# Two linear-attention blocks mixed by a gate, on one core: weight loads, W' work and denominator work placed differently around the last transposes

## The chip, the cores and the metric

The kernel runs on one NeuronCore of one Trainium2 chip. The metric is device microseconds for one execution. TensorE (PE in the profile; its weight loads are PEld) does the matrix products, VectorE (DVE) and ScalarE (ACT) the elementwise work, GpSimd (POOL) some memsets, and the sync engine (SP) issues nearly all DMAs from one in-order queue (SPq).

## The reference, cut to what matters

Two blocks A and B have the same input `x` (2048 x 640, bf16) and weights of their own. `phi` is an ELU-like feature map, H is 32 heads of 20 columns.

```python
x = A_x
g = _sigmoid((x * gate_w).sum(-1, keepdims=True))
qkv = x @ wqkv;  q, k, v = three parts, 32 heads of 20
phi = lambda t: jnp.where(t > 0, t + 1, jnp.exp(t)) + 1e-6
pq, pk = phi(q), phi(k)
kv = jnp.einsum("bhsd,bhse->bhde", pk, v)
z = jnp.einsum("bhsd->bhd", pk)
num = jnp.einsum("bhqd,bhde->bhqe", pq, kv)
den = jnp.einsum("bhqd,bhd->bhq", pq, z)[..., None] + 1e-6
a = (num / den).reshape(B, S, D) @ wo        # and b likewise, with B's weights
return g * a + (1 - g) * b
```

## The kernel before, in words

**Stages.** (1) k-units: for each of 16 row tiles, `x` times both k weights (L557, L558), then exp, relu and add on ACT and DVE. (2) Five g-units (`g_unit`, L814): G = pkᵀx for both blocks in seven products of eight matmuls each, P1 to P7 (L806), with a Strassen-like combination on DVE and ACT; beside them runs the query work of the row blocks 0 and 1 (`q_unit`, L762). A row block is 512 rows; there are four. Each g-unit ends with two DMA transposes, `gsA` and `gsB`, from the tile WKW into GSA and GSB. (3) `kv_unit` (L924): G times the v weights gives the per-head kv; three masked copies on DVE (L904) make the tile KVL. (4) `wp_burst` (L957): kv times `wo` gives W' for each block in two halves; each half leaves PSUM by two copies of 124 x 960 (L972), and after the second half five DMAs store W' to DRAM (`st`, L988), and one DMA (`wplA`, `wplB`) loads it back in the order in which the output products need it. (5) Output: for each of 16 row tiles, 20 matmuls (L1116; the first ten read A's W', the others B's), a copy (L1140) and a store.

**The denominator.** For each row block b, `t_sum` (L1007) adds up, on DVE, five products of query features with z per attention block: the first is a multiply-add (L1016, g = 0), the others take the sum so far along (L1022). `den(b)` (L1031) then transposes the sums by DMA (`tt`), reduces them (L1049), takes the reciprocal (L1061), multiplies by the gate and spreads each factor over four columns in one instruction (L1064), transposes that back by DMA (`fx`) and scales the query features in two halves (L1094, "pqs"). Output tiles 4b to 4b+3 need pqs of block b.

**What sets the order.** The kernel is written as a list of operations with dependencies, and a planner (`Sched.run`, L99) places them at build time: on each engine it takes the operation that can start first by its own cost figures, and among those that can start, the one with the lowest `prio`. `prio` is the place in the program's text unless it is given; the weight loads discussed here have −1. PE is the exception: its operations stay in the order of the text. At run time every engine and the SP queue work through that fixed order, each instruction behind the one in front of it. The first loads carry a `behind` link (L370) that keeps them in order among themselves; `can` (L110) refuses an operation whose `behind` has not been placed. An operation with no dependencies can start at the planner's first moment, 300 ns, like the first load of `x`.

**Placing of the loads and of the query work.** `fill_g` (L1174) is called four times within each g-unit (k = 0 to 3). In the last g-unit it calls `load_wv` at k = 0 (v weights A and B, 800 KB each, waiting for the products P1 and P2, whose tiles they overwrite), and `load_wo` at k = 1 (eight DMAs, 1650 KB together, waiting for P6 and P2). Query units 2 and 3 of the row blocks come as ten "double" units of two PSUM banks each (two exps and relus of 1024 columns, L784 and L785; L788 and L794 on DVE). L1193 to L1222 set their order: two doubles, kv, one, W' A half 0, one, `den(1)`, W' A half 1, one, W' B half 0, one, W' B half 1, three, the first products of two output tiles, one more double inside the output loop, then `den(2)`, `den(3)`. `den(0)` stands ahead of all of these.

Of the kernel before, what the change touches and what calls it, by code (L numbers as in the profile page):

```python
# [42 lines left out]
HC = 320  # L43
RELUB = (3, 5, 7, 9, 11, 13)
QPRE = 2
QO = 3
NEA = 2
QFILL = ((3, 2, 1, 1), (0, 1, 1, 1), (0, 1, 1, 1), (0, 1, 1, 1), (0, 1, 1, 0))

# [222 lines left out]
def body(nc, A_x, A_wqkv, A_wo, B_x, B_wqkv, B_wo, gate_w, out, log=None):  # L272
# [26 lines left out]
    ONE = sb("ONE", [128, 2], bf)  # L299
    SCR = sb("SCR", [128, 1], f32)  # L300
    EPSC = sb("EPSC", [128, 1], f32)
    IDN = sb("IDN", [128, 128], bf)
    PS = nc.alloc_psum_tensor("ps", [128, 8, 512], f32)

# [23 lines left out]

    base = RA1 * RL
    WVW = D + 28  # L330
    WV = {X: PKf[:, base + i * NC * WVW : base + (i + 1) * NC * WVW].rearrange("p (c f) -> p c f", c=NC) for i, X in enumerate(XS)}
    base += 2 * NC * WVW
    WO = {X: PKf[:, base + i * NU * D : base + (i + 1) * NU * D].rearrange("p (u f) -> p u f", u=NU) for i, X in enumerate(XS)}
    assert base + 2 * NU * D <= (RS2 + 1) * RL
    PQ23 = PKf[:, RS1 * RL : RS1 * RL + 4 * 2560].rearrange("p (b k s) -> p b k s", b=2, k=10)
# [47 lines left out]
    def dve2(n):  # L383
        return 150 + 0.53 * n
# [12 lines left out]

    op("DVE", lambda e: e.memset(ONE[:, :], 1.0), 60.0, outs=[bone], name="one")
    sch.consts = [op("POOL", lambda e: e.memset(EPSC[:, :], EPS), 100.0, outs=[beps], name="eps")]
    op("ACT", lambda e: e.activation(SCR[:, :], EPSC[:, :], ACT.Exp), 1500.0, ins=[beps], outs=[bge0], prio=10**6, name="table")  # L400
    bid = Buf("idn")
    op(
# [49 lines left out]
    loading.clear()  # L452

    bpad = {X: Buf("pad") for X in XS}

    def load_wv(after):
        for X in XS:
            for lo, hi in ((0, 4), (D + 4, D + 28)):
                op("POOL", lambda e, X=X, lo=lo, hi=hi: e.memset(WV[X][:, :, lo:hi], 0.0), 300.0, outs=[bpad[X]], after=after, name="wvpad")
            dma("SP", "wv" + X, WV[X][:, :, 4 : D + 4], w3(X, 2), 819200, outs=[bwv[X]], after=after, prio=-1)  # L460

    def load_wo(after):
        for X in XS:
            for r in range(2):
                bwo[X, r] = Buf("wo")
                dma(
                    "SP",
                    "wo%s%d" % (X, r),
                    WO[X][4 + HR * r : 64 + HR * r, 0:5, :],
                    wo[X][0:600, :].rearrange("(u r p) n -> r p u n", r=2, p=HR)[r],  # L470
                    384000,
                    outs=[bwo[X, r]],
                    after=after,
                    prio=-1,
                )
            bwo[X, 2] = Buf("wo")
            dma("SP", "wopad" + X, WO[X][0:4, 0:5, :], wo[X][0:4, :].unsqueeze(1).to_broadcast([4, 5, D]), 25600, outs=[bpad[X]], after=after, prio=-1)
            dma("SP", "wo2" + X, WO[X][64:104, 5, :], wo[X][600:640, :], 51200, outs=[bwo[X, 2]], after=after, prio=-1)

    bw = Buf("warm", "ps")  # L480

# [266 lines left out]

    bpq = {}

    def q_unit(b, slots):
# [33 lines left out]
        op("ACT", lambda e: e.activation(dst, pv(), ACT.Relu), act_cost(512 * n), ins=[ps], outs=[rq], after=pq_free[b], name="qr")  # L785
# [8 lines left out]
        op("DVE", lambda e: e.tensor_tensor(out=dst, in0=dst, in1=ev(), op=ALU.add), dve2(512 * n), ins=[rq, eq, eq2], outs=[pq], name="qs")  # L794

    bgs = {}
    bz = {}
    last = {}
    pq_free = {0: [], 1: [], 2: [], 3: []}
# [14 lines left out]
    def g_unit(g, fill):  # L814
# [62 lines left out]
        op("ACT", lambda e: e.activation(GT[:, gb.slot, 0:HC], PS[:, px.slot, 0:HC], ACT.Copy), act_cost(HC), ins=[px], outs=[gb], name="c21")  # L877
        for X, b in (("A", ga), ("B", gb)):
            bgs[X, g] = Buf("gs%s%d" % (X, g))
            dma(  # L880
                "SP",
                "gs%s%d" % (X, g),
                GS[X][:, :, 128 * g : 128 * g + 128],
                lambda b=b: GT[:, b.slot, :],
                163840,
                ins=[b],
                outs=[bgs[X, g]],
                issue=1250.0,
                transpose=True,
                prio=-2,  # L890
            )
# [52 lines left out]
    def wp_burst(X, half):  # L944
# [18 lines left out]
                        )  # L963
            return x

        op("PE", fn, 640.0, ins=bkvl[X] + [bwo[X, i] for i in range(3)] + [bpad[X]], outs=ps, name="wp%s%d" % (X, half))
        for r in range(2):
            dst = WST[X][0:124, 3 * r : 3 * r + 3, lo : lo + HALF]
            src = lambda r=r: psw(ps[r], 3 * HALF)[0:124, :].rearrange("p (k n) -> p k n", k=3)
            op(  # L970
                "ACT",
                lambda e, dst=dst, src=src: e.activation(dst, src(), ACT.Copy),  # L972
                act_cost(3 * HALF),
                ins=[ps[r]],
                outs=[bwst[X, r]],
                prio=-1,
                name="wpc",
            )
# [28 lines left out]
    def t_sum(X, b, g):  # L1007
# [5 lines left out]
        n = Buf("ts")  # L1013
        after = []
        if g == 0:
            f = lambda e: e.tensor_scalar(acc, src, z, EPS / 4, op0=ALU.mult, op1=ALU.add)  # L1016
            prev = []
            if b >= 2:
                after.append(ts_last[X, b - 2])
# [11 lines left out]
    def den(b):  # L1031
# [30 lines left out]
        ff_op[b] = op(  # L1062
            "DVE",
            lambda e: e.tensor_tensor(  # L1064
                out=FF[:, s, :].rearrange("p (t h j) -> p t h j", t=8, j=4),
                in0=DNT[:, s, :].rearrange("p (t h) -> p t h", t=8).unsqueeze(3).to_broadcast([128, 8, H, 4]),
                in1=GG[:, b, :, :].rearrange("p x t -> p (x t)").unsqueeze(2).unsqueeze(3).to_broadcast([128, 8, H, 4]),
                op=ALU.mult,
            ),
            dve1(1024),  # L1070
            ins=[b3, bgg, bgg2],
            outs=[b4],
            after=[ft_op[old]] if b >= 2 else [],
            name="ff",
        )
        ft_op[b] = dma(
            "SP",
            "fx%d" % b,
# [87 lines left out]
                t_sum(X, b, ts[X, b])  # L1166
                ts[X, b] += 1

    def q_next(n):
        for _ in range(n):  # L1170
            if qs:
                q_unit(*qs.pop(0))
# [91 lines left out]
```

## Time and profile before

Time: median 198.56 us of 3 runs (197.31 to 198.69). The profiled execution took 198.07 us, of which its span, from the first to the last instruction, is 196.7 us.

| | |
|---|---|
| profiled execution, device time | 198.07 us |
| its span | 196.7 us |
| PE busy | 181.2 us (92%) |
| DVE busy | 135.4 us (69%) |
| ACT busy | 105.9 us (54%) |
| DMA moved | 21.37 MB, 109 GB/s mean |
| last g-unit ends on PE; kv begins | 113.0 us; 117.55 us |
| first output product; last DVE scaling (pqs) begins | 142.29 us; 181.96 us |

A line of the timeline or of the chain begins with the start in us and the length in us; then come engine, line of the kernel, operation and tiles, and in brackets the idle time before it with what ended it. PEclk is the granted TensorE clock as a part of full speed. A line of the waits gives the total in us, the number of waits and the longest. "us to landing" is the time from a DMA's issue to its last byte. A line of the table by stage gives the stretch, its length, then the busy time of PE, PEld, DVE, ACT and POOL with the number of instructions, then PEclk, the share of DMA engine time, and GB/s.

### The profile page before, as it was taken

What the parts mean: (1) busy time and instruction counts of PE and PEld (TensorE: products, weight loads), DVE (VectorE), ACT (ScalarE), POOL (GpSimd) and SP (SyncE); (2) the same over time, 40 slices, a digit from 0 to 9 for tenths busy, and PEclk for the clock granted to TensorE, in tenths of its full rate; (3) what the DMA queues carried; (4) which work ended last, traced back from release to release, by engine and by line L of the source; (5) the groups of instructions that cost most, each with busy time, mean ns of one, the idle gap of its engine ahead of it and who ended that gap; (6) DMA issues with size and microseconds to landing.
All of it is one profiled execution on the core that took longest, in us unless ns stands there. A gap on an engine that the chain in (4) does not pass through costs nothing.

```text
span 196.7 us, 3099 instructions
## 1 busy us (share of the span) xinstructions
PE 181.2 (92%) x1235; PEld 114.2 (58%) x1257; DVE 135.4 (69%) x230; ACT 105.9 (54%) x177; POOL 1.2 (1%) x12
## 2 busy tenths in 40 slices
PE   9999999999999999999999909978954999999995
PEld 4555555555666777777787509444522555555552
DVE  2388969889898727282865717969999799543500
ACT  4279888888675536343534530599732722222222
POOL 1000000000000000000000000000000000000000
PEclk9999999999999999999999975999996999999999
DMA  7979998000000303014139993096665124264122
GB/s 199 285 139 141 268 375 264 6 0 3 0 0 0 70 0 67 0 38 32 27 71 354 206 196 68 0 131 182 167 182 168 37 81 107 72 84 120 67 72 67
DMA packets 36245, 21.37 MB, mean 109 GB/s; under 512 B 25438, under 2 KB 35974, under 8 KB 36230
## 3 DMA queue, kind: packets, MB, share of 16 engines
q1 hardware_dynamic: 35932, 20.97, 45.1%
q8 instruction: 10, 0.16, 0.4%
q10 hardware_dynamic: 298, 0.20, 0.3%
q14 instruction: 5, 0.04, 0.1%
HBM read 10.87 MB, written 4.26 MB: 77 GB/s over the span
## 4 chain that ended last, share of the span: by engine, by line
PE 81%; DMA 8%; ACT 6%; DVE 1%; issue 1%; SPq 0%; DVEq 0%; ACTq 0%
PE ps L1116 21%; PE ps L806 18%; PE ps L557 17%; PE ps L762 15%; PE ps L558 5%; DMA GSA<-WKW 5%; ACT TX L972 3%; PE ps L924 3%; DMA PKS<-wpsB 2%; ACT EQ L784 2%; ACT PKS L785 2%; PE ps L486 1%; DMA wpsB<-TX 1%; PE ps L499 1%; DVE WKW L833 0%
## 5 line engine op out<-in xcount | busy, mean ns | idle before, releaser
L557 PE MATMUL ps<-WKW,XT 128*128 128x512 bf16 x154 | 43.8, 386 | 0.0
L784 ACT ACTIVATE EQ<-ps 128x512 bf16<-128x512 f32 (+1 forms) x30 | 22.5, 750 | 38.3 <-PE ps L762 31.6
L558 PE MATMUL ps<-WKW,XT 128*128 128x128 bf16 (+1 forms) x160 | 35.5, 222 | 0.3
L1116 PE MATMUL ps<-PKS,PQ 128*128 128x512 bf16 (+1 forms) x157 | 23.0, 307 | 5.3 <-DMA PKS<-wpsB 5.2
L557 PEld LDWEIGHTS ps<-WKW,XT 128*128 128x128 bf16 x160 | 15.9, 100 | 19.3 <-issue 0.8
L1140 ACT ACTIVATE TX<-ps 128x640 bf16<-128x640 f32 (+1 forms) x16 | 11.2, 698 | 28.4 <-PE ps L1116 28.4
L597 ACT ACTIVATE EKT<-ps 128x640 bf16<-128x640 f32 x32 | 22.3, 704 | 6.9 <-PE ps L558 6.3
L762 PE MATMUL ps<-XT,WQA 128*128 128x512 bf16 x95 | 22.8, 380 | 2.3 <-ACT PKS L785 2.2
L806 PE MATMUL ps<-TX,PKS 128*128 128x321 bf16 (+1 forms) x160 | 24.6, 300 | 0.0
L762 PE MATMUL ps<-XT,WQB 128*128 128x512 bf16 x95 | 22.8, 379 | 0.3
L1116 PE MATMUL ps<-PKS 128*128 128x128 bf16 (+1 forms) x157 | 21.7, 298 | 0.2
L806 PEld LDWEIGHTS ps<-TX,PKS 128*128 128x128 bf16 x160 | 18.8, 117 | 5.0
L1116 PEld LDWEIGHTS ps<-PKS,PQ 128*128 128x128 bf16 x160 | 12.8, 101 | 15.2 <-DMA PKS<-wpsB 5.1
L788 DVE TENSOR_SCALAR EQ<-EQ 128x512 bf16<-128x512 bf16 (+1 forms) x30 | 10.0, 333 | 15.9 <-ACT EQ L784 15.8
L806 PE MATMUL ps<-XN,PKS 128*128 128x321 bf16 (+1 forms) x120 | 18.0, 300 | 0.0
L1116 PEld LDWEIGHTS ps<-PKS 128*128 128x128 bf16 x160 | 12.3, 98 | 9.7 <-DVE PKS L1094 0.3
L762 PEld LDWEIGHTS ps<-XT,WQA 128*128 128x128 bf16 x100 | 11.5, 119 | 10.6 <-ACT PKS L785 2.4
L762 PEld LDWEIGHTS ps<-XT,WQB 128*128 128x128 bf16 x100 | 11.6, 118 | 8.2 <-issue 0.2
L558 PEld LDWEIGHTS ps<-WKW,XT 128*128 128x128 bf16 x160 | 15.9, 100 | 0.0
L806 PEld LDWEIGHTS ps<-XN,PKS 128*128 128x128 bf16 x120 | 14.1, 117 | 3.1
L610 ACT ACTIVATE PKS<-ps 128x640 bf16<-128x640 f32 x20 | 14.0, 699 | 0.0
L828 ACT ACTIVATE EKT<-ps 128x321 f32<-128x321 f32 (+1 forms) x15 | 6.6, 439 | 11.2 <-PE ps L806 11.1
(60 smaller groups left out, 191.3 us busy)
## 6 DMA issues: line engine op xcount, KB each, us to landing
out_dram<-TX SPq DMA_DIRECT2D x15, 160.0 KB, 1.8
XN<-in_A_x_dram SPq DMA_DIRECT2D x1, 2240.0 KB, 9.5
WKW<-in_A_wqkv_dram SPq DMA_DIRECT2D x5, 160.0 KB, 3.8
WKW<-in_B_wqkv_dram SPq DMA_DIRECT2D x5, 160.0 KB, 3.8
WQA<-in_A_wqkv_dram SPq DMA_DIRECT2D x1, 800.0 KB, 11.1
WQB<-in_B_wqkv_dram SPq DMA_DIRECT2D x1, 800.0 KB, 13.8
PKS<-in_A_wqkv_dram SPq DMA_DIRECT2D x1, 800.0 KB, 4.6
PKS<-in_B_wqkv_dram SPq DMA_DIRECT2D x1, 800.0 KB, 6.8
```

What stands on the lines that cost most here:

```text
L557: e.matmul(a[:, 0:512], l, WK[X][:, c, 0:512], start=(c == 0), stop=(c == NC - 1))
L558: return e.matmul(a[:, 512:w], l, WK[X][:, c, 512:w], start=(c == 0), stop=(c == NC - 1))
L597: op("ACT", lambda e, i=i, ps=ps: e.activation(ev(i), psw(ps, D), ACT.Exp), act_cost(D), ins=[ps] + first, outs=[ek, b], name="ke")
L610: op("ACT", lambda e, X=X, ps=ps: e.activation(pkt(X, t), psw(ps, D), ACT.Relu), act_cost(D), ins=[ps], outs=[rk], name="kr")
L762: r = e.matmul(PS[:, ps.slot + i, :], WQ[X][:, c, g::5], XT[:, c, 512 * b : 512 * b + 512], start=(c == 0), stop=(c == NC - 1),)
L784: op("ACT", lambda e: e.activation(ev(), pv(), ACT.Exp), act_cost(512 * n), ins=[ps], outs=[eq], name="qe")
L788: lambda e: e.tensor_scalar(ev(), ev(), 1.0, EPS, op0=ALU.min, op1=ALU.add),
L806: r = e.matmul(PS[:, ps.slot, 0:w], PKS[:, reg, j, g::5], mov(j, w), start=(first and j == 0), stop=(j == 7), skip_group_check=not first)
L828: return op("ACT", lambda e: e.activation(PT[:, dst.slot, 0:w], PS[:, ps.slot, 0:w], ACT.Copy), act_cost(w), ins=[ps], outs=[dst], after=e ...
L924: r = e.matmul(PS[0:n, ps.slot, GR * i : GR * i + NC * w], WV[X][:, c, lo : lo + n], gv[:, c, :, 24 * u : 24 * u + w], start=(c == 0), sto ...
L1116: r = e.matmul(a[:, l0 - lo : h0 - lo], PQ[b][:, NC * XS.index(X) + g, 128 * (t % 4) : 128 * (t % 4) + 128], WP[X][:, g, l0:h0], start=(X ...
L1140: op("ACT", lambda e: e.activation(OST[:, os_.slot, 0:w], psw(ps, w), ACT.Copy), act_cost(w), ins=[ps], outs=[os_], name="oc")
```

## The change

- **v weights.** A's get a tile of their own (`WVA`) and their load is written into the second g-unit with no dependencies; B's stay in the last g-unit and wait for P1 alone.
- **`wo`.** The eight loads move from k = 1 to k = 3 of the last g-unit, and a `behind` link puts them after the last `gsB` transpose in SP's order. Their padding gets a buffer name of its own (`bpo`), so that kv no longer waits for it.
- **W' and queries.** Between each two W' bursts there is still one double; after the last burst come four instead of three, and none is left in the output loop. `den(0)` moves to before W' B half 0, `den(1)` to after W' B half 1, `den(2)` and `den(3)` to before the output.
- **Two of the eight W' copies** (A, second of each half) go from ACT to DVE (`WPDVE`).
- **First z sums** (g = 0, all four row blocks, both blocks: eight) go from DVE to ACT as an activation with a per-row scale and bias (`TSACT`).
- **Factor expansion** for row blocks 1, 2, 3: DVE multiplies 256 factors by the gate, and ACT spreads them over 1024 columns (`FFACT`).
- The new switch `relu` of `q_unit` keeps its old value in every call (`QR` is "ACT").

```diff
-QO = 3
+TSACT = (0, 1, 2, 3)
+FFACT = (1,2,3)
+WPDVE = (("A", 0, 1), ("A", 1, 1))
+QR = "ACT"
...
-    WV = {X: PKf[:, base + i * NC * WVW : base + (i + 1) * NC * WVW].rearrange("p (c f) -> p c f", c=NC) for i, X in enumerate(XS)}
-    base += 2 * NC * WVW
+    WV = {"A": sb("WVA", [128, NC, WVW], bf), "B": PKf[:, base : base + NC * WVW].rearrange("p (c f) -> p c f", c=NC)}
+    base += NC * WVW
...
+    sch.consts.append(op("POOL", lambda e: e.memset(EPQ[:, :], EPS / 4), 100.0, outs=[beps], name="epq"))
...
-    def load_wv(after):
-        for X in XS:
+    bpo = {X: Buf("pad") for X in XS}
+
+    def load_wv(X, after):
+        if X:
             for lo, hi in ((0, 4), (D + 4, D + 28)):
                 op("POOL", lambda e, X=X, lo=lo, hi=hi: e.memset(WV[X][:, :, lo:hi], 0.0), 300.0, outs=[bpad[X]], after=after, name="wvpad")
             dma("SP", "wv" + X, WV[X][:, :, 4 : D + 4], w3(X, 2), 819200, outs=[bwv[X]], after=after, prio=-1)
...
+                o.behind = gs_last[0]
...
-        op("PE", fn, 640.0, ins=bkvl[X] + [bwo[X, i] for i in range(3)] + [bpad[X]], outs=ps, name="wp%s%d" % (X, half))
+        op("PE", fn, 640.0, ins=bkvl[X] + [bwo[X, i] for i in range(3)] + [bpo[X]], outs=ps, name="wp%s%d" % (X, half))
...
+            if (X, half, r) in WPDVE:
+                op("DVE", lambda e, dst=dst, src=src: e.tensor_copy(dst, src()), dve1(3 * HALF), ins=[ps[r]], outs=[bwst[X, r]], prio=-1, name="wpc")
+            else:
+                op("ACT", lambda e, dst=dst, src=src: e.activation(dst, src(), ACT.Copy), act_cost(3 * HALF), ins=[ps[r]], outs=[bwst[X, r]], prio=-1, name="wpc")
...
         if g == 0:
+            if b >= 2:
+                after.append(ts_last[X, b - 2])
+            if b in TSACT:
+                op(
+                    "ACT",
+                    lambda e: e.activation(acc, src, ACT.Identity, bias=EPQ[:, :], scale=z),
...
+        if b in FFACT:
+            b5 = Buf("fm")
+            op(
+                "DVE",
+                lambda e: e.tensor_tensor(
+                    out=DNT[:, s, :].rearrange("p (t h) -> p t h", t=8),
+                    in0=DNT[:, s, :].rearrange("p (t h) -> p t h", t=8),
+                    in1=GG[:, b, :, :].rearrange("p x t -> p (x t)").unsqueeze(2).to_broadcast([128, 8, H]),
+                    op=ALU.mult,
+                ),
...
+            ff_op[b] = op("ACT", lambda e: e.activation(fv, dv, ACT.Copy), act_cost(1024), ins=[b5], outs=[b4], after=old_ft, name="ff")
...
     def fill_g(g):
         def f(k):
+            if g == 1 and k == 0:
+                load_wv("A", [])
             if g == 4 and k == 0:
-                load_wv([last["P1"], last["P2"]])
-            if g == 4 and k == 1:
+                load_wv("B", [last["P1"]])
+            if g == 4 and k == 3:
                 load_wo([last["P6"], last["P2"]])
...
     ts_ready()
-    den(0)
     q_next(2)
     kv_unit("A")
     kv_unit("B")
     q_next(1)
     wp_burst("A", 0)
     q_next(1)
-    den(1)
     wp_burst("A", 1)
     q_next(1)
-    ts_ready()
+    den(0)
     wp_burst("B", 0)
     q_next(1)
     wp_burst("B", 1)
-    q_next(QO)
+    den(1)
+    q_next(1)
+    ts_ready()
+    q_next(1)
+    q_next(1, QR)
+    ts_ready()
+    den(2)
+    q_next(1, QR)
+    ts_ready()
+    den(3)
```

More of the change, by code (lines that the diff above doesn't have):

```diff
@@ L301, in body @@
     EPSC = sb("EPSC", [128, 1], f32)
+    EPQ = sb("EPQ", [128, 1], f32)
     IDN = sb("IDN", [128, 128], bf)
@@ L465, in load_wo @@
                 bwo[X, r] = Buf("wo")
-                dma(
+                o = dma(
                     "SP",
@@ L475, in load_wo @@
                 )
+                o.behind = gs_last[0]
             bwo[X, 2] = Buf("wo")
-            dma("SP", "wopad" + X, WO[X][0:4, 0:5, :], wo[X][0:4, :].unsqueeze(1).to_broadcast([4, 5, D]), 25600, outs=[bpad[X]], after=after, prio=-1)
-            dma("SP", "wo2" + X, WO[X][64:104, 5, :], wo[X][600:640, :], 51200, outs=[bwo[X, 2]], after=after, prio=-1)
+            o = dma("SP", "wopad" + X, WO[X][0:4, 0:5, :], wo[X][0:4, :].unsqueeze(1).to_broadcast([4, 5, D]), 25600, outs=[bpo[X]], after=after, prio=-1)
+            o.behind = gs_last[0]
+            o = dma("SP", "wo2" + X, WO[X][64:104, 5, :], wo[X][600:640, :], 51200, outs=[bwo[X, 2]], after=after, prio=-1)
+            o.behind = gs_last[0]
     bw = Buf("warm", "ps")
@@ L749, in body, with q_unit @@
     bpq = {}
-    def q_unit(b, slots):
+    def q_unit(b, slots, relu="ACT"):
         n = len(slots)
@@ L784, in q_unit @@
         op("ACT", lambda e: e.activation(ev(), pv(), ACT.Exp), act_cost(512 * n), ins=[ps], outs=[eq], name="qe")
-        op("ACT", lambda e: e.activation(dst, pv(), ACT.Relu), act_cost(512 * n), ins=[ps], outs=[rq], after=pq_free[b], name="qr")
+        if relu == "ACT":
+            op("ACT", lambda e: e.activation(dst, pv(), ACT.Relu), act_cost(512 * n), ins=[ps], outs=[rq], after=pq_free[b], name="qr")
         op(
@@ L793, in q_unit @@
         )
-        op("DVE", lambda e: e.tensor_tensor(out=dst, in0=dst, in1=ev(), op=ALU.add), dve2(512 * n), ins=[rq, eq, eq2], outs=[pq], name="qs")
+        if relu == "ACT":
+            op("DVE", lambda e: e.tensor_tensor(out=dst, in0=dst, in1=ev(), op=ALU.add), dve2(512 * n), ins=[rq, eq, eq2], outs=[pq], name="qs")
+        else:
+            op(
+                "DVE",
+                lambda e: e.scalar_tensor_tensor(dst, pv(), 0.0, ev(), op0=ALU.max, op1=ALU.add),
+                dve1(512 * n),
+                ins=[ps, eq, eq2],
+                outs=[pq],
+                after=pq_free[b],
+                name="qs",
+            )
     bgs = {}
+    gs_last = [None]
     bz = {}
@@ L879, in g_unit @@
             bgs[X, g] = Buf("gs%s%d" % (X, g))
-            dma(
+            gs_last[0] = dma(
                 "SP",
@@ L969, in wp_burst @@
             src = lambda r=r: psw(ps[r], 3 * HALF)[0:124, :].rearrange("p (k n) -> p k n", k=3)
[L970 to L978, printed above, removed]
+            if (X, half, r) in WPDVE:
+                op("DVE", lambda e, dst=dst, src=src: e.tensor_copy(dst, src()), dve1(3 * HALF), ins=[ps[r]], outs=[bwst[X, r]], prio=-1, name="wpc")
+            else:
+                op("ACT", lambda e, dst=dst, src=src: e.activation(dst, src(), ACT.Copy), act_cost(3 * HALF), ins=[ps[r]], outs=[bwst[X, r]], prio=-1, name="wpc")
             if half == 0:
@@ L1015, in t_sum @@
         if g == 0:
+            if b >= 2:
[4 more added lines that the diff above has]
+                    lambda e: e.activation(acc, src, ACT.Identity, bias=EPQ[:, :], scale=z),
+                    act_cost(512),
+                    ins=[bz[X, g], bpq[b, NC * i + g]],
+                    outs=[n],
+                    after=after,
+                    name="ts0",
+                )
+                bts[X, b] = n
+                return
             f = lambda e: e.tensor_scalar(acc, src, z, EPS / 4, op0=ALU.mult, op1=ALU.add)
             prev = []
-            if b >= 2:
-                after.append(ts_last[X, b - 2])
         else:
@@ L1061, in den @@
         op("DVE", lambda e: e.reciprocal(DNT[:, s, :], DNT[:, s, :]), 150 + 6.26 * 256, ins=[b2], outs=[b3], name="rc")
[L1062 to L1075, printed above, removed]
+        dv = DNT[:, s, :].rearrange("p (t h) -> p t h", t=8).unsqueeze(3).to_broadcast([128, 8, H, 4])
+        fv = FF[:, s, :].rearrange("p (t h j) -> p t h j", t=8, j=4)
+        old_ft = [ft_op[old]] if b >= 2 else []
+        if b in FFACT:
+            b5 = Buf("fm")
+            op(
+                "DVE",
+                lambda e: e.tensor_tensor(
[4 more added lines that the diff above has]
+                ),
+                dve1(256),
+                ins=[b3, bgg, bgg2],
+                outs=[b5],
+                name="fm",
+            )
+            ff_op[b] = op("ACT", lambda e: e.activation(fv, dv, ACT.Copy), act_cost(1024), ins=[b5], outs=[b4], after=old_ft, name="ff")
+        else:
+            ff_op[b] = op(
+                "DVE",
+                lambda e: e.tensor_tensor(
+                    out=fv, in0=dv, in1=GG[:, b, :, :].rearrange("p x t -> p (x t)").unsqueeze(2).unsqueeze(3).to_broadcast([128, 8, H, 4]), op=ALU.mult
+                ),
+                dve1(1024),
+                ins=[b3, bgg, bgg2],
+                outs=[b4],
+                after=old_ft,
+                name="ff",
+            )
         ft_op[b] = dma(
@@ L1167, in ts_ready, with q_next @@
                 ts[X, b] += 1
-    def q_next(n):
+    def q_next(n, relu="ACT"):
         for _ in range(n):
             if qs:
-                q_unit(*qs.pop(0))
+                q_unit(*qs.pop(0), relu)
     def fill_g(g):
         def f(k):
+            if g == 1 and k == 0:
+                load_wv("A", [])
             if g == 4 and k == 0:
-                load_wv([last["P1"], last["P2"]])
-            if g == 4 and k == 1:
+                load_wv("B", [last["P1"]])
+            if g == 4 and k == 3:
                 load_wo([last["P6"], last["P2"]])
```

## The prediction

> **What bounds the kernel now.** I read the waits first, then the chain that ended last, then the table by stage. PE is busy 92% of the span, so what matters is where it stands still, and what keeps its work from coming earlier. The waits (total us, number, longest):
>
> ```profile
> DVE XN L1049 <- DMA XN<-XN: 9.4, 2, 4.7
> PE ps L1116 <- DMA PKS<-wpsB: 5.2, 1, 5.2
> PE ps L924 <- DMA GSA<-WKW: 4.6, 1, 4.6
> DVE PKS L1094 <- DMA XN<-XN: 3.1, 1, 3.1
> DVE PQ L1094 <- DMA XN<-XN: 1.5, 1, 1.5
> PEld ps L1116 <- DVE PKS L1094: 0.3, 1, 0.3
> ```
>
> PE has two long stalls: kv waits 4.6 us for the last transpose of A's G, and the first product with B's W' waits 5.2 us for the load of W'. The last line looks harmless but decides this case: at 183 us PE waits for DVE's scaling of the last row block. It is only 0.3 us because DVE arrives just then. The chain names the same two transfers:
>
> ```profile
> 107.72 9.70 DMA GSA<-WKW
> ...
> 117.55 5.12 PE ps L924 x60
> ...
> 142.93 2.42 DMA wpsB<-TX
> ...
> 145.43 4.46 DMA PKS<-wpsB
> 149.88 0.45 issue
> 150.33 2.45 PE ps L1116 x9
> ```
>
> The stages:
>
> ```profile
> 2.00:4.00 2.00, 2.00 (x14) 1.34 (x13) 0.97 (x3) 1.20 (x4) 0.00 (x0) 1.00 0.96 271
> 103.00:105.00 2.00, 1.95 (x13) 1.36 (x13) 0.07 (x1) 1.13 (x3) 0.00 (x0) 1.00 1.03 382
> 109.00:111.00 2.00, 2.00 (x11) 1.09 (x10) 2.00 (x4) 0.28 (x2) 0.00 (x0) 1.00 1.27 210
> 111.00:113.00 2.00, 1.91 (x9) 0.82 (x7) 0.74 (x3) 1.78 (x2) 0.00 (x0) 1.00 1.05 209
> 118.84:169.93 51.09, 43.52 (x324) 25.40 (x329) 47.06 (x58) 26.11 (x30) 0.00 (x0) 0.94 0.43 107
> 124.90:139.30 14.40, 12.17 (x105) 6.43 (x104) 12.60 (x14) 14.34 (x16) 0.00 (x0) 1.00 0.60 133
> ```
>
> The v weights move at 382 GB/s, the `wo` loads behind them at 210. From 118.84 to 169.93 us, where the sums of the last row block end, DVE is busy 47.06 of 51.09 us: a second bound beside PE. In the W' bursts ACT is full (14.34 of 14.40 us).
>
> **The first stall.** The last gsA is issued at 107.72 us and lands after 9.7 us; the other four take 2.6. It queues behind `wo` (A's landing after 7.6 us, B's after 10.9). With `wo` behind gsB, gsA lands at 107.72 + 2.6 = 110.3 and gsB, issued at 109.2 once its ACT copy ends, at about 112. PE has its two doubles until 112.96, so kv starts at 113.0 instead of 117.55. Its 60 matmuls took 5.12 us, at PEclk 0.50 until 122; without the stall they need between half and all of that, I take 3.6. W' A half 0 then comes after one double (2.16) at 118.8 instead of 124.78: **6.0 us earlier**. `wo` is late next: issued from 110.4, with a fixed 2.5 us (4.6 to land 800 KB, 2.14 of it at 382 GB/s) and 1650 KB at 209 GB/s, A's half arrives at 117.0, B's at 121.0. Both are in time (B's is needed at about 124), but `tt0` queues behind them and lands at about 121.9, against 118.8 before.
>
> **The W' bursts.** ACT needed 12.5 us from the third double's exp (124.95) to the last W' copy (137.45). Two copies go (0.92 apart, 1.84 off), one or two z sums come. The trace has no such activation: the 128x512 exp took 0.60 us, the 128x640 copy 0.70; I take 0.65. So 118.95 + 12.5 − 1.84 + 0.65 = 130.3. The Trainium skill ("ScalarE: Activation LUTs", section "What ACT_TABLE_LOAD costs") gives such an instruction 186 ns + 0.833 ns per element + 93 ns for each per-row operand, 0.80 us by my estimate, and its rules for kernel authors put multiply and add on VectorE; by it ACT would lose 0.15 us more for each sum. Store and load of B's W' took 9.4 us from the first store (140.48) to landing (149.88); the stores had waited 3.0 us on SP behind an `fx` transpose. From 130.3 this gives 139.7, or 142.7 behind a transpose. PE gets there, with four doubles (8.6) after the last burst and two tiles of A's products (2.7), at about 139.5. The second stall goes, or shrinks to 3 us.
>
> **DVE.** It stood still from 114.1 to 118.84 with rd0 (L1049) at the head of its queue, waiting for `tt0`. Now `den(0)` is written later, so kv's masked copies and query work stand ahead of rd0, and DVE can work on from 114.1. The work up to the end of block 3's sums, in mean durations, before: nine doubles at 1.11 (10.0), kv copies 4.24, three factor chains at 4.19 (1.22 + 1.75 + 1.22), three scalings at 2.89, sums 13.5: 49.0, which took 51.1 with its waits, a factor of 1.043. After: 10.0 + 4.24 + two W' copies 2.3 (a PSUM read of 640 took 0.82, of 480 1.50; I take 1.15 for 960, bounds 0.82 and 3.0 each) + 4.19 + two chains at 3.39 (the gate multiply of 256: 0.29 to 0.49 by the smallest 128- and 320-column rows, 0.42 taken) + two scalings 5.77 (the third falls into the wait for the last transpose) + 16 sums at 0.75 (12.0) = 45.3, times 1.043 = 47.2. So the sums end at 114.1 + 47.2 = 161.3 instead of 169.93. From there to block 3's first scaling it took 13.5 us (4.6 transpose, 1.22, 1.75, 1.22, 3.2 transpose, 1.48); the handover to ACT adds 0.42 + 1.05 (as 128x1024 exp, 1.02 to 1.06) + 0.2 for two crossings − 1.22 = 0.45. First scaling done: **161.3 + 13.95 = 175.3**, instead of 183.44.
>
> From that point before, four output tiles and the tail took 196.67 − 183.44 = 13.23 us. The new end, without the next part, is 188.5 us: 8.2 us gained. PE alone could have gained 4.6 + 1.5 (kv at full clock) + 2.2 (waits for ACT) + 5.2 + 1.2 (half of 149.4 to 152.7, PEclk 0.50) = 14.7; DVE keeps 6.5 of them.
>
> **The early load.** A's v load has no dependencies, no `behind` link and `prio` −1. Where its call stands in the text doesn't hold it: at the planner's first moment it competes with the first load of `x` and wins. So 800 KB go to the head of SP's queue, in front of what PE waits for:
>
> ```profile
> 0.00 0.40 SPq L366 DMA_DIRECT2D XN<-in_A_x_dram  x1
> 0.46 2.32 SPq L366 DMA_DIRECT2D WKW<-in_A_wqkv_dram  x5
> 2.69 1.23 PE L499 MATMUL ps<-IDN,XN 128*128 128x128 bf16 x10
> 3.71 0.63 PE L557 MATMUL ps<-WKW,XT 128*128 128x512 bf16 x1
> ```
>
> PE transposes the first row tile as soon as it lands (2.6 us). 819,200 B cost 2.14 us at 382 GB/s and 3.0 at the 271 of that stage; 1.6 if the slow first half microsecond hides some. PE then idles between warm-up and first transpose. From its start at 0.3 its 512-column matmuls take 0.63 us, from 5.9 on 0.38; a column pair takes 0.54, then 0.27. If the slow phase starts anew, up to 2 us more pass at half rate: 0 to 1.0, I take 0.4. The skill's page "TensorE: Matmul & The Clock Gate" (Part 1) has a free-running window of 3.4 us that must be busy; by it I estimate the extra at 0 to 1.7 us, by chance of phase; the records (0.50 from 115 to 122) fit such windows. Everything after shifts along, for PE is without a gap until 113. I take **+2.5 us**, bounds 1.6 and 4.0.
>
> **Costs at nothing.** Four z sums in the g-units: ACT is busy 30.27 of 59 us there; if one stood ahead of a copy that a product waits for, 0.3 us. The memsets on POOL: idle. WVB one product earlier: nothing waits for it.
>
> **The sum.** 196.7 − 8.2 + 2.5 = 191.0 us span; the profiled execution has 1.4 us around it: 192.4, against its own 198.07 (median of the runs 198.56).
>
> **Rivals.**
> (A) *PE bound.* DVE keeps up because its order fits better: 196.7 − 14.7 + 2.5 + 1.4 = **185.9**. For it: DVE has 4 us of waits in that stretch. Against: the sum above has them only in proportion, and 12 us of sums must follow the queries. Chance 0.13.
> (B) *Slower: DVE waits in order for the factor handover.* Multiply, ACT spread, SP transpose, scaling now cross three engines for blocks 1 to 3, and if the planner, which prices the transposes lower, puts the scaling (L1094) right behind the multiply, DVE stands for 1.05 + 3.1 to 4.7 us each time with sums queued behind. Block 3's is in my sum; blocks 1 and 2 add 8.3 to 11.5: **200.7 to 203.9**. It is slower than before from 5.7 us of added waits on. For it: DVE has waited like this (4.7, 1.5, 3.1). Against: there is other ready work until the queries end. Chance 0.16.
> (C) *Half of it.* `wo` or rd0's wait holds W' or DVE as before, and 4 us of the 8.2 remain: **196.6**, at the bound to no change. Chance 0.12.
> (D) *The early load isn't at the front,* so the start is unchanged: **189.9**. Against: the planner's rule. Chance 0.07.
> The forecast has 0.52.
>
> **Numbers.** About 1% (196.6 to 200.5) is what measurement can't tell from no change. Faster by more: 0.52 + 0.13 + 0.07 and a little of (C), less for what I may not see: 0.72; within: 0.11; slower: 0.17. The range takes in the start's bounds (1.5 us up), the W' copies' (3.7 up), the upper half of (A) and the low end of (B), and leaves out under 0.2: 186 to 201.
>
> **What will show it.** Right: A's v load first on SP, first PE transpose near 4.8 us; gsA's last landing within 3 us; kv without a stall at about 115.5; DVE without a gap of 4 us after it; the last scaling near 178, with PE waiting for it (L1116 behind L1094) by some us. Wrong: output products without any gap (A); DVE waiting several times for XN transposes at L1094 (B); the first `x` landing at 2.6 us as before (D).

## The result, and the profile after

The changed kernel takes **196.27 us** (median of 20 runs, 194.94 to 198.9); the kernel before took 198.55 (median of 20, 196.62 to 199.46). The ratio is 0.990, 95% interval 0.987 to 0.992: 1% faster, where 3% were forecast. Its profiled execution took 196.41 us, its span 195.0, so it stands for the median. For two of the experiments below (all W' copies on ACT, all z sums on DVE) the one profiled execution was an unusually slow one, so only their times are read.

The waits of the changed kernel (total us, number, longest); its lines L508, L979, L993, L1078, L1140 and L1162 are L499, L957, L972, L1049, L1094 and L1116 of the kernel before:

```profile
DVE PKS L1140 <- DMA XN<-XN: 6.0, 2, 4.3
...
PE ps L979 <- DVE TX L993: 4.4, 1, 4.4
...
DVE XN L1078 <- DMA XN<-XN: 3.4, 1, 3.4
...
PE ps L508 <- DMA XN<-in_A_x_dram: 3.1, 1, 3.1
...
PE ps L1162 <- DVE PKS L1140: 2.0, 1, 2.0
...
DVE PQ L1140 <- DMA XN<-XN: 1.9, 1, 1.9
```

Both long stalls of before, 4.6 us for A's last transpose and 5.2 for B's W', are gone. In their place PE waits 3.1 us at the start, 4.4 at the second W' burst for a copy on DVE, and 2.0 for a scaling. The timeline of the first six microseconds (start, length, engine and line, idle time before) shows the first of them:

```profile
0.00 0.46 SPq L370 DMA_DIRECT2D WVA<-in_A_wqkv_dram  x1
0.52 0.51 SPq L370 DMA_DIRECT2D XN<-in_A_x_dram  x1
...
5.91 1.23 PE L508 MATMUL ps<-IDN,XN 128*128 128x128 bf16 x10 [3.07 <-DMA XN<-in_A_x_dram]
```

A's v load is the first on SP's queue, and the first transposes on PE begin at 5.91 us instead of 2.69. The two double queries ahead of kv begin at 111.52 us instead of 108.48: of the 3.22 us, 3.04 stay to there. (The 113.0 us in the table of the kernel before is where these doubles end; the last products of its g-units ended at 108.65.) Then the last transposes and kv, on SP and PE:

```profile
110.75 1.40 SPq L370 DMA_TRANSPOSE GSA<-WKW  x1
112.20 1.28 SPq L370 DMA_TRANSPOSE GSB<-WKW  x1
113.53 1.79 SPq L370 DMA_DIRECT2D PKS<-in_A_wo_dram  x4
```

```profile
115.84 1.59 PE L946 MATMUL ps<-GSA,WVA 128*128 128x120 bf16 x30
117.28 1.59 PE L946 MATMUL ps<-GSB,PKS 128*128 128x120 bf16 x30
...
121.53 0.61 PE L979 MATMUL ps<-PKS 64*60 64x320 bf16 x15 [0.48 <-DMA PKS<-in_A_wo_dram]
122.75 2.35 PE L771 MATMUL ps<-XT,WQB 128*128 128x512 bf16 x10 [0.61 <-DVE PKS L926]
129.47 1.01 PE L979 MATMUL ps<-PKS 64*60 64x320 bf16 x15 [4.36 <-DVE TX L993]
```

kv begins straight after the doubles, without a wait, and in spite of the late start 1.7 us earlier than before. The first W' burst is 3.3 us earlier (121.53 against 124.78). But the second is at 129.47, 4.36 us later than PE could have done it. What it waits for stands in DVE's timeline:

```profile
122.73 0.75 DVE L1051 SCALAR_TENSOR_TENSOR WKW<-PKS,ZC,WKW 128x512 f32<-128x512 bf16 x1
126.92 1.22 DVE L1078 TENSOR_REDUCE XN<-XN 128x256 f32<-128x1024 bf16 x1 [3.43 <-DMA XN<-XN]
128.17 1.16 DVE L993 CAST TX<-ps 124x960 bf16<-124x960 f32 x1
```

rd0 (L1078) again stands still for its transpose `tt0`, as before, and now the first W' copy on DVE (L993) is queued right behind it. The copy's input has been in PSUM since 122.1 us and holds the banks that the second burst needs. The chain that ended last runs through that place:

```profile
115.19 0.81 PE ps L771 x3
...
116.96 9.94 DMA XN<-XN
126.92 1.22 DVE XN L1078
128.17 1.17 DVE TX L993
129.47 1.01 PE ps L979 x15
```

`tt0` is issued at 116.96 us behind the eight `wo` loads and lands 9.94 us later. The stall has a second price, which the table by stage shows (stretch, length, busy time of PE, PEld, DVE, ACT, POOL, then PEclk):

```profile
118.84:169.93 51.09, 43.82 (x296) 23.18 (x299) 42.27 (x55) 29.18 (x35) 0.00 (x0) 0.93 0.59 135
128.34:135.16 6.82, 5.34 (x32) 2.19 (x37) 6.72 (x9) 2.13 (x3) 0.00 (x0) 0.50 0.37 98
```

PE is at half clock for 6.82 us, from 128.34, still within the stand, to 135.16. In the stretch that was compared before, DVE is now busy 42.27 of 51.09 us (47.06 before): less work, but not done earlier.

### The profile page after: what moved, and what is told of

Its sections match the earlier page's. It is cut to its first block, busy times and chain, and to the rows that moved or that the text cites. A ratio compares the mean times of both kernels' runs of the same rounds, so it can differ in the third digit from the quotient of the medians.

```text
span 195.0 us, 3101 instructions
## 1 busy us (share of the span) xinstructions
PE 180.2 (92%) x1235; PEld 112.3 (58%) x1257; DVE 131.6 (67%) x224; ACT 112.4 (58%) x186; POOL 1.2 (1%) x13
## 4 chain that ended last, share of the span: by engine, by line
PE 70%; DMA 12%; DVE 9%; ACT 6%; issue 2%; SPq 0%; DVEq 0%
PE ps L828 20%; PE ps L566 17%; PE ps L771 15%; PE ps L1162 11%; DMA XN<-XN 9%; PE ps L567 5%; DMA XN<-in_A_x_dram 3%; DVE WKW L1051 3%; ACT TX L995 2%; ACT PKS L795 2%; DVE PQ L1140 1%; ACT EQ L793 1%; DVE XN L1078 1%; DVE XN L1090 1%; DVE PKS L1140 1%
## 5 line engine op out<-in xcount | busy, mean ns | idle before, releaser
L771 PE MATMUL ps<-XT,WQB 128*128 128x512 bf16 x95 | 23.9, 392 | 0.9 <-DVE PKS L926 0.6
L771 PE MATMUL ps<-XT,WQA 128*128 128x512 bf16 x95 | 23.5, 390 | 1.0 <-ACT EQ L793 0.5
L1162 PE MATMUL ps<-PKS 128*128 128x128 bf16 (+1 forms) x157 | 21.6, 297 | 2.1 <-DVE PKS L1140 2.0
L1162 PE MATMUL ps<-PKS,PQ 128*128 128x128 bf16 (+1 forms) x157 | 21.7, 297 | 0.2
L1162 PEld LDWEIGHTS ps<-PKS 128*128 128x128 bf16 x160 | 12.3, 98 | 11.6 <-DVE PKS L1140 2.1
L1162 PEld LDWEIGHTS ps<-PKS,PQ 128*128 128x128 bf16 x160 | 12.3, 98 | 9.5
```

Of the source, the lines that this page charges most:

```text
L771: r = e.matmul(PS[:, ps.slot + i, :], WQ[X][:, c, g::5], XT[:, c, 512 * b : 512 * b + 512], start=(c == 0), stop=(c == NC - 1),)
L1162: r = e.matmul(a[:, l0 - lo : h0 - lo], PQ[b][:, NC * XS.index(X) + g, 128 * (t % 4) : 128 * (t % 4) + 128], WP[X][:, g, l0:h0], start=(X ...
```

## Experiments

Ratios below are to the kernel before, timed beside each of them, so 0.990 is the changed kernel itself; brackets have the 95% interval. None of them leaves out any of the computation.

### The early load

Two runs: the load put back, and the load alone.

```diff
-            dma("SP", "wv" + X, ..., prio=-1)
+            o = dma("SP", "wv" + X, ..., prio=-1)
+            if X == "A":
+                o.behind = chain["SP"]        # behind the last of the first loads
```

> The changed kernel with one edit: A's v load keeps its own tile but is linked behind the last of the first loads, so that x and the k weights are first in SP's queue again. The order on PE, ACT and DVE stays as in the changed kernel but for a few neighbours on DVE. Theory of the start (the load at the head of the queue costs 3.0 us and nothing else): first transpose on PE at 2.7 us instead of 5.9, kv's first matmul near 112.8 instead of 115.84, time 193.3 us, all of the 3.0 us kept to the end. Rival (DMA work late in the kernel has a clock of its own, and PE only waits longer there): first transpose at 2.7, but rd0's wait for its transpose and PE's stall before the second W' burst grow, time 195 to 196.4.

Measured: 192.16 us, ratio 0.977 (0.972 to 0.982). The first transposes are at 2.76 us and kv at 112.62 instead of 115.84. The rest of the path keeps its shape: PE still waits 3.83 us for DVE's copy at the second burst.

```diff
 # the kernel before, and in it only:
+            if g == 1 and k == 0:
+                load_wv("A", [])              # tile of its own
-                load_wv([last["P1"], last["P2"]])
+                load_wv("B", [last["P1"]])
```

> The kernel before with one part of the change alone: A's v weights in a tile of their own, loaded without dependencies, B's behind the sixth gradient's product as in the change. Queue theory (the load goes to the head of SP's queue and everything behind it moves along): first PE transpose at 5.9 us instead of 2.69, the start costs 3.0 us. The load that is gone from the end of the g-units lets `wo` and the last transpose of A's G start earlier by at most the 2.1 us that 800 KB take at 382 GB/s, so kv's wait of 4.6 us shrinks to 2.5 to 4.6. Time 199.5 to 201.6, ratio 1.005 to 1.015, slower. Rival (the load is hidden, as PE waits for other loads of the start anyway): first transpose before 4 us, time 196.4 to 199, ratio 0.99 to 1.00.

(B's load waits for the product P1, as the edit has it.) Measured: 200.16 us, ratio 1.016 (1.010 to 1.021), slower; the profiled execution was the quickest of six, 199.16. From the timeline of PE:

```profile
6.10 1.23 PE L499 MATMUL ps<-IDN,XN 128*128 128x128 bf16 x10 [3.27 <-DMA XN<-in_A_x_dram]
```

```profile
118.64 2.68 PE L924 MATMUL ps<-GSA,WVA 128*128 128x120 bf16 x30 [2.17 <-DMA GSA<-WKW]
```

The start is late, and the load that left the end of the g-units shortens kv's wait from 4.59 to 2.17 us. These 2.42 us are two thirds of the 3.51 that are lost up to the doubles (111.99 against 108.48). The rival, a load that hides, is out. Over all kernels of this study whose profiles are read, the two doubles ahead of kv begin between 111.52 and 112.27 us in the six with this load at the front, and between 107.82 and 108.52 in the six without: the means are 111.95 and 108.23, so the early load costs **3.7 us** at that point, where I had 2.5. At the end of the changed kernel it costs less: 0.977 against 0.990 is 1.3%, or 2.5 us.

### `wo` behind the last transposes

```diff
 # the kernel before, and in it only:
+                o.behind = gs_last[0]         # on each wo load, with pad buffers of their own
-            if g == 4 and k == 1:
+            if g == 4 and k == 3:
                 load_wo([last["P6"], last["P2"]])
```

> The kernel before with one part alone: the `wo` loads behind the last transpose of B's G, one double later, in their own pad buffers; v loads, rd0's place, z sums, W' copies and factor chain as before. Theory that the time of `tt0` decides (rd0 stands in DVE's queue in front of what PE needs): gsA's last landing within 3 us, kv at about 113 without its wait of 4.6 us, but `wo` and, behind it, `tt0` land 3 to 4 us later than before (122 instead of 118.8), DVE stands at rd0 until then with kv's masked copies behind it, and the first W' burst waits for them: at most 1 us is gained or lost, 197.5 to 199.5, ratio 0.995 to 1.005. Rival (the removed wait is kept, as my forecast had it): 6 us on W' A, 193 to 195, ratio 0.97 to 0.98.

Measured: 196.12 us, ratio 0.990 (0.986 to 0.993), between the two theories. On PE and on DVE:

```profile
112.35 1.59 PE L929 MATMUL ps<-GSA,PKS 128*128 128x120 bf16 x30
...
117.52 0.60 PE L962 MATMUL ps<-PKS 64*60 64x320 bf16 x15
```

```profile
122.51 1.22 DVE L1054 TENSOR_REDUCE XN<-XN 128x256 f32<-128x1024 bf16 x1 [2.71 <-DMA XN<-XN]
```

kv starts 5.2 us earlier and the first burst 7.3. I was wrong that kv's masked copies would be behind rd0: DVE had done them. rd0, which waits for `tt0`, begins 3.7 us later (118.84 before), as both theories had it. Of the 7.3 us only 2.1 (1% of 198) are left at the end. In the profile PE then waits 2.35 us for a relu on ACT, 1.21 for A's W' and 3.96 for B's.

### The rest alone

```diff
 # the changed kernel, with the loads where the kernel before has them:
-            if g == 1 and k == 0:
-                load_wv("A", [])
             if g == 4 and k == 0:
-                load_wv("B", [last["P1"]])
-            if g == 4 and k == 3:
+                load_wv("A", [last["P1"], last["P2"]])
+                load_wv("B", [last["P1"], last["P2"]])
+            if g == 4 and k == 1:
                 load_wo([last["P6"], last["P2"]])     # no behind link
```

> The changed kernel without its two moves of loads: A's and B's v loads and `wo` where the kernel before has them; z sums on ACT, factor expansion on ACT, two W' copies on DVE, single double queries between the bursts and the later den(0) remain. If the parts add up (early load alone 1.0155, `wo` alone 0.990, all 0.990), the rest alone gives 0.985: 194 to 195.5, ratio 0.980 to 0.988. PE's first stall of 4.6 us remains, the second (5.2 before) shrinks. Rival (the rest pays only where the first stall is gone): 0.993 to 1.00.

Measured: 194.62 us, ratio 0.986 (0.982 to 0.990). As expected, PE's first stall stays (4.66 us) and the second shrinks, to 1.91. The parts add up: 1.0155 x 0.9896 x 0.9857 = 0.991, and the whole change has 0.990. By the three intervals such a product is good to some 0.8%, so effects of the parts on one another of that size are not excluded. Two of the members of the rest were put back one at a time.

```diff
-TSACT = (0, 1, 2, 3)
+TSACT = ()
```

> The changed kernel with all first z sums back on DVE (8 of 0.81 us on ACT become 8 of 0.5 to 0.75 on DVE, four of them in the g-units). Theory that the chain of block 2 (its scaling at 169.47 us, PE waiting 2.04 for it) is set by the stand at rd0 and then by DVE's work: four sums more lie ahead of it, of which part falls into DVE's waits: its scaling 0.5 to 2 us later, time 196.3 to 198.3, ratio 0.990 to 1.00, against 0.990 with them on ACT. Rival (ACT is the bound in the W' bursts, so sums of 0.81 us there cost PE): the second burst is no later and the time falls by 0.5 to 1.5 us, ratio 0.982 to 0.987.

Measured: 200.24 us, ratio 1.002 (0.996 to 1.009), slower than I expected.

```diff
-FFACT = (1,2,3)
+FFACT = ()
```

> The changed kernel with the factor's expansion back on DVE in all blocks (three chains get 0.8 us more of DVE and lose the two crossings, 0.45 us each in the chain's length). Theory that the handover is not what holds block 2's scaling: time within 0.7 us of the changed kernel's, 195.6 to 197, ratio 0.986 to 0.994. Rival (B of the prediction: the handover between engines holds DVE): DVE's waits at L1140 of 6.0 us fall by 2 or more and the time by 1.5 to 3 us, ratio 0.975 to 0.982.

Measured: 197.0 us, ratio 0.995 (0.992 to 0.998). So the z sums on ACT bring about 2.4 us (1.2% of 198) and the factor expansion about 1 (0.5%, at the edge of the two intervals). Both rivals, that ACT or the handover pays for them, are out in this kernel. For the z sums the time is shown, not the place where it is won.

### The stand at rd0

Four kernels take the W' copy or rd0 out of the other's way. First, all W' copies back on ACT, and rd0 and rd1 put by hand behind both DVE copies:

```diff
-WPDVE = (("A", 0, 1), ("A", 1, 1))
+WPDVE = ()
```

> The changed kernel with the two W' copies given back to ACT; nothing else is edited. Theory of the queue: no copy stands behind rd0, so PE's stall of 4.4 us before the second W' burst goes; rd0 still waits about 3.4 us on DVE, with query work behind it, while DVE has 2.3 us less to do: the end 1 to 3 us earlier, 193.5 to 195.5 us. Rival of the handover: PE's stall goes, the end stays at 196 us. If moving the copies helped as it was meant to (ACT full in the bursts), the bursts take some 2 us longer and the time is 197 to 198.

Measured: 195.14 us, ratio 0.989 (0.986 to 0.992).

```diff
+        if b < 2:
+            red_op[b].behind = wpd[-1]        # the last W' copy on DVE
```

> The changed kernel with one edit: the reduces of row blocks 0 and 1 (rd0, rd1) may be placed on DVE only behind the second of the two W' copies that DVE took over. DMAs and their order stay. Theory of the queue (the copy stood behind rd0, rd0 waited 3.4 us for a transpose that had landed late behind the wo loads, and PE waited 4.4 us for the PSUM banks of that copy): PE's stall before the second W' burst under 0.5 us, no half clock there, DVE's wait at rd0 under 1 us as sums and copies fill it, the scaling of block 2 and the end 2.5 to 3.5 us earlier: 193 to 194 us. Rival of the handover (the factor chains of blocks 1 to 3 over DVE, ACT, SP and DVE set the end): the stall goes, but the scalings of blocks 2 and 3 come less than 1 us earlier, time 195.5 to 196.4.

Measured: 195.84 us, ratio 0.988 (0.983 to 0.993). Neither differs from the changed kernel by what can be measured: moving the two copies to DVE brings nothing that shows, and the 193 to 194 us that I expected of rd0 put late did not come. In the profile with rd0 put late the wait at the second burst is down from 4.36 to 1.27 us, and another has come:

```profile
127.11 0.61 PE L980 MATMUL ps<-PKS 64*60 64x320 bf16 x15 [1.27 <-DVE TX L994]
...
142.48 1.52 PE L1165 MATMUL ps<-PKS,PQ 128*128 128x512 bf16 x10
147.88 7.35 PE L1165 MATMUL ps<-PKS,PQ 128*128 128x128 bf16 x44 [3.87 <-ACT EQ L793]
```

The output products begin 4.8 us earlier than in the changed kernel and then stand for 3.87 us, for an exp of a double query on ACT. What holds ACT is seen on DVE and ACT:

```profile
140.35 2.90 DVE L1143 TENSOR_TENSOR PQ<-PQ,XN 128x2560 bf16<-128x2560 bf16 x2 [2.33 <-DMA XN<-XN]
...
144.30 0.42 DVE L1101 TENSOR_TENSOR XN<-XN,GG 128x256 f32<-128x256 f32 x1
```

```profile
144.75 1.06 ACT L1112 ACTIVATE XN<-XN 128x1024 bf16<-128x1024 f32 x1 [3.09 <-DVE XN L1101]
145.71 0.80 ACT L1039 ACTIVATE WKW<-PKS,EPQ,ZC 128x512 f32<-128x512 bf16 x1
146.42 1.92 ACT L793 ACTIVATE EQ<-ps 128x1024 bf16<-128x1024 f32 x2
```

DVE waits 2.33 us at block 0's scaling for its transpose, which follows from the later rd0; block 1's gate multiply (L1101) is behind that; ACT's expansion (L1112) waits 3.09 us for the multiply, and the exp that PE needs is queued behind the expansion. This is the mechanism of rival (B), with ACT in place of DVE as the engine that is held. In the changed kernel ACT waits for the multiply as well (3.4 us for block 2's, 1.1 for block 3's), but then only copies of the output stand behind the expansion.

Next, the planner was given a rate of 205 bytes per ns for the four large `wo` loads (375 KB each) instead of its 330, and nothing else. In the trace of the changed kernel DMA moves 199 GB/s from 118 to 120 us and 205 from 120 to 122, while these loads run.

```diff
                 o.behind = gs_last[0]
+                o.dma = (o.dma[0], o.dma[1], 205.0, o.dma[3])
```

> The changed kernel with one number changed: the rate at which the planner believes the `wo` loads to move is set to the 205 B/ns that this profile shows. Theory that the planner put rd0 in front of the W' copy since it held `tt0` to land some us earlier than it does: with the true rate rd0 stands behind the first DVE copy, PE's wait of 4.36 us at the second burst falls below 2 us. What follows is as with rd0 placed by hand behind both copies (0.988): 194 to 196, ratio 0.980 to 0.990. Rival (the placing doesn't matter, DVE stands at rd0 as long from another place): the wait for the second burst remains at 3 us or more, ratio 0.990.

Measured: 194.14 us, ratio 0.981 (0.977 to 0.986). The planner now puts two more sums and the first W' copy in front of rd0, and rd0 waits for nothing:

```profile
123.18 2.33 DVE L1052 SCALAR_TENSOR_TENSOR WKW<-PKS,ZC,WKW 128x512 f32<-128x512 bf16 x3
125.52 1.16 DVE L994 CAST TX<-ps 124x960 bf16<-124x960 f32 x1
126.60 0.42 DVE L799 TENSOR_SCALAR EQ<-EQ 128x1024 bf16<-128x1024 bf16 x1
126.93 1.21 DVE L1079 TENSOR_REDUCE XN<-XN 128x256 f32<-128x1024 bf16 x1
```

rd0 begins at the same time as in the changed kernel (126.93 against 126.92), but DVE has worked through the 3.4 us in front of it. This one number is worth 0.8%, and it is what made the planner place the wait where it hurt. It fits the size of the stand: at 330 bytes per ns their 1500 KB take 4.7 us, at 205 they take 7.5, 2.8 us more, and the stand was 3.43.

Last, `tt0` in front of the `wo` loads on SP's queue:

```diff
-                o.behind = gs_last[0]
+                wo_ops.append(o)
...
     den(0)
+    for o in wo_ops:
+        o.behind = tt_op[0]
```

> The changed kernel with one edit: the wo loads are linked behind the transpose tt0 instead of the last gsB, so that tt0 goes first in SP's queue. Theory of the queue: tt0 lands near 116.5 instead of 126.8 us, rd0 no longer waits; the wo loads start 1.3 us later, so that the first W' burst waits 2 us instead of 0.5; net gain 2 to 3 us: 193.5 to 194.5. Rival of the handover: the later W' bursts cost what rd0 wins, time 196 to 197.

Measured: 192.89 us, ratio 0.980 (0.976 to 0.984). rd0 runs at 117.14 us without a wait, ahead of kv's masked copies; the first two bursts wait 0.91 us for `wo` and 1.40 for a copy, and the clock is recorded as full throughout.

### Both repairs together

The load late, and either the true rate or `tt0` first:

> A's v load linked behind the last load of the start, and the planner told 205 B/ns for the `wo` loads. If the placing of rd0 costs what the load doesn't, 0.970 to 0.975 (192); if W' B's way through memory takes the stall over, as with rd0 placed by hand, 0.975 to 0.980, no better than the late load alone (0.977).

Measured: 189.86 us, ratio 0.961 (0.957 to 0.965).

> Two repairs of the changed kernel together: A's v load linked behind the last load of the start (alone 0.977 of the kernel before), and the `wo` loads behind `tt0` in SP's queue (alone 0.980). The first returns the 3 us of the start, the second lets rd0 run before kv's masked copies and takes the stand of DVE (3.43) and PE (4.36) away. If the two are independent, each takes 1 to 1.3% off the changed kernel's 0.990: ratio 0.965 to 0.970, 191 us, first transpose at 2.8, rd0 at about 114 without a wait, no wait of 3 us or more of PE on DVE's W' copy, span about 189. Rival (with the stall gone the same bound lies behind both: W' B's way through memory and block 2's scaling): no better than the better of the two, 0.975 to 0.98.

Measured: **188.75 us**, ratio 0.955 (0.952 to 0.958), the best of all: 4.5% faster than the kernel before and 3.5% faster than the changed one (0.9548 / 0.9898 = 0.965). Both are better than expected, and the rival (the same bound behind both repairs) is out. PE in the second of them:

```profile
118.43 0.61 PE L982 MATMUL ps<-PKS 64*60 64x320 bf16 x15 [1.08 <-ACT EQ L795]
...
122.53 0.61 PE L982 MATMUL ps<-PKS 64*60 64x320 bf16 x15 [1.20 <-ACT EQ L795]
...
140.10 1.53 PE L1165 MATMUL ps<-PKS,PQ 128*128 128x512 bf16 x10 [0.67 <-ACT PKS L797]
143.00 19.19 PE L1165 MATMUL ps<-PKS,PQ 128*128 128x512 bf16 x140 [1.38 <-DMA PKS<-wpsB]
163.38 21.91 PE L1165 MATMUL ps<-PKS 128*128 128x512 bf16 x160 [1.19 <-DVE PKS L1143]
```

No wait of PE behind kv is longer than 1.4 us; ACT, W' B's load and DVE's scaling each hold it once or twice for about a microsecond. PE is busy 96% of this span. By the single runs I expected 0.967 for the two together; the further 1% I have not taken apart. That is not shown to be the clock, but it may have a part: only `tt0` first and these two show a mean granted clock of 1.0 over their profiled executions.

## Why the prediction was wrong, point by point

The forecast was 192.4 us, the median is 196.3; in the profiled executions, a span of 191.0 against 195.0. The time stands at rival (C), which had 196.6 and a chance of 0.12, and so does the mechanism: rd0's wait holds W' and DVE as before.

**The step that failed** is in the part on DVE: "kv's masked copies and query work stand ahead of rd0, and DVE can work on from 114.1". They do stand ahead of it, but they and one sum last only until 123.5 us, and `tt0` lands at 126.9. I had worked out 121.9 for `tt0` (124.4 with the start), and did not ask what work was left ahead of rd0 at that moment, nor what stood behind it. Behind it stood the first W' copy that the same change had just moved to DVE. DVE stood 3.43 us, PE 4.36. In this profile block 3's sums end at 167.76 us, where 161.3 + 2.5 = 163.8 was forecast; the 4.0 us between are 3.43 of this stand and 0.54 of a later start, and the end is 4.0 us late as well.

That the stand is what failed is seen where it is gone. These are the ends of block 3's sums on DVE in the changed kernel, with the planner's rate corrected, and with that and the load late:

```profile
166.35 1.41 DVE L1051 SCALAR_TENSOR_TENSOR XN<-PKS,ZC,WKW 128x512 bf16<-128x512 bf16 x2
163.43 1.42 DVE L1052 SCALAR_TENSOR_TENSOR XN<-PKS,ZC,WKW 128x512 bf16<-128x512 bf16 x2
159.97 1.42 DVE L1054 SCALAR_TENSOR_TENSOR XN<-PKS,ZC,WKW 128x512 bf16<-128x512 bf16 x2
```

Against the forecast's 161.3, moved by what each profile had lost or gained at the doubles:

| kernel | doubles against before | 161.3, moved | sums end | DVE's wait at rd0 |
|---|---|---|---|---|
| changed | +3.04 | 164.3 | 167.76 | 3.43 |
| load late | −0.17 | 161.1 | 162.67 | 2.90 |
| planner's rate | +3.51 | 164.8 | 164.85 | none |
| `tt0` first | +3.59 | 164.9 | 164.61 | none |
| load late and planner's rate | +0.04 | 161.3 | 161.39 | none |
| load late and `tt0` first | −0.66 | 160.6 | 160.16 | none |

Without the stand the sum for DVE holds within 0.5 us. (With the load late alone, a stand of 2.90 us leaves the sums only 1.5 late; I have not taken that apart.) Some of that is luck: from 117.14 us, which is 114.1 and the 3.04, to the end of the sums DVE worked 43.49 us in the changed kernel where I had 45.3, and its waits other than the stand were 3.7 us where the factor allowed 1.9. (The work before was added up as 49.0 too, where the row of the stage has 47.06 busy.) The reason for the placing was the planner's rate for `wo`, which I had in front of me as a row of the trace (209 GB/s) and used for the landing, but not for the question what the planner believes.

**The first stall: right.** The last gsA was issued at 110.75 us, and nothing was left to wait for when kv began at 115.84. The 60 matmuls, at full clock, took 3.0 us (115.84 to 118.87), against 3.6 taken.

**The early load: right in place, too small in size.** It is first on SP, and later work moved along. The term was 2.5 us; at the doubles it was 3.0 in this profile (the first transposes were 3.22 late and 0.2 of it was regained, where 0.4 more had been taken for the clock) and 3.7 by the means over twelve, inside the bounds of 1.6 to 4.0. At the end of this kernel the times give 2.5.

**`wo` and `tt0`.** The first burst had to wait for `wo`, but only 0.48 us. `tt0` was 2.5 us later than forecast, 0.5 of it from the start.

**The W' bursts.** With the load late and the true rate, the last W' copy on ACT ends at 131.8 us; the sum had 130.3. In the changed kernel itself the stand puts it at 140.3. The second stall of before is gone, as forecast, also since PE comes to it late.

**The durations.** The z sum on ACT took 0.81 to 0.89 us, where I took 0.65; the estimate of 0.80 from the Trainium skill ("ScalarE: Activation LUTs", section "What ACT_TABLE_LOAD costs") was the better one. The advice of that page to keep multiply and add on VectorE (section "Rules for kernel authors") is given for the speed of the engine, and there the trace agrees: 0.48 us on DVE for the same size. As a rule for placing the work it does not hold here, where moving eight such sums off DVE is worth 1.2%. The gate multiply was taken at 0.42 and took 0.42, the W' copy on DVE at 1.15 and took 1.13, the expansion on ACT at 1.05 and took 1.08.

**The bound.** DVE's scaling does set the end, but PE waits for block 2's (2.04 us at 171.24), not block 3's. Block 3's first half ends at about 181.5 us (180.00 and half of 2.90), 13.7 us after its sums, where 13.95 was worked out, and just in time.

**The rivals.** (A), PE alone: no; even in the best experiment, with no wait over 1.4 us, the ratio is 0.955 where (A) had 0.936. (B), the handover: not at its price, as DVE waits 1.93 and 1.71 us at the scalings of blocks 1 and 2 where (B) had 4.2 to 5.8 each; but a chain of its kind held PE when rd0 was put late. (D), the load not at the front: no; but its number can be looked at with the load moved back. It was 189.9, or 0.956 of the kernel before. With the load alone moved back the ratio is 0.977, with the planner's rate corrected too 0.961 (0.957 to 0.965), though the last waits of PE there (2.20 us for ACT, 1.05 for block 2's scaling) are not quite those of the sum. So the forecast comes within 0.5% of the kernel whose planner knows how long its loads take, and not of this one.

**What stays open.** The span of the profiled execution was missed by 4.0 us. With the planner's rate corrected it is 192.5 instead of 195.0, so 2.5 of the 4.0 go with the stand (by the medians 0.8%, 1.7 us), and 1.0 of the rest is that profile's start (3.51 us at the doubles, where I had 2.5). The path to the end is not quite the forecast's there either: PE goes into the last products at 168.49 us without a wait for a scaling, but has waited 2.19 for an exp on ACT. What would give way next at that point has no run of its own. Nor has the reason why the price of the early load at the end differs: 1.3% in the changed kernel, 2.1% with the rate corrected (0.961 / 0.981), 2.6% with `tt0` first (0.955 / 0.980).

## What to carry to other kernels

When an instruction waits for a DMA in an in-order queue, ask three things: when the DMA lands, how much work is queued ahead of the instruction, and what stands behind it. The last is what turns an idle microsecond into a stall, and it matters most where the same change moves new work onto that engine. If the order comes from a build-time planner, compare its rates with the trace for exactly those transfers whose landing decides the order; one wrong rate cost 0.8% here. And in a planner like this one a load without dependencies or links goes to the front of its queue: "early" has to be said relative to the loads that the start needs.

## What the hardware showed that I had not expected

- **The clock at the start is full after a time that varies.** A 512- and a 128-column matmul together take 0.54 us up to some moment and 0.27 after it, twice the rate. (PEclk has 1.00 in these first microseconds, as in the row 2.00:4.00 of the table by stage, so this is read from the matmuls themselves.) Of two kernels whose first 512-column matmuls begin at 6.92 and 6.85 us, the one reaches the full rate at 8.97, the other at 9.98; with the load late another begins at 3.78 and reaches it at 4.29. Of the six kernels with A's v load at the front, one came to the two doubles ahead of kv 0.75 us later than another.
- **A long stand of PE goes with a half-clock stretch of one of two lengths.** With the stand of 4.36 us it was 6.82 us (0.50 from 128.34 to 135.16), with 3.87 us and rd0 put late 3.41 us (0.50 from 146.92 to 150.33), with 3.83 us and the late load 3.41 us (0.50 from 127.13 to 130.54). In these three it begins between 1.1 us before the end of the stand and 1.4 after it. The length of the stand alone does not decide: with the planner's rate corrected a stand of 2.19 us has half clock from 146.42 to 149.84, and with the late load as well one of 2.20 us has none. In the two other kernels whose clock stayed full the longest stands behind kv were 1.43 and 1.38 us. Half clock for 6.82 us, with PE busy 5.34 of it, is worth up to some 2.7 us of PE's work on top of the stand, by my estimate.
